# Merging the 64-row query tiles of two heads in an attention and MLP kernel

## The chip, the core and the metric

The kernel runs on one NeuronCore of a Trainium2 chip. The metric is the time of the whole program on the device in microseconds (us). Before the change the median of 3 runs is 1101.58 us.

## The reference

Attention over 4 batches, 8 heads, 576 tokens and 64 features, with a second, memory branch, then two feed-forward layers over all 2304 tokens.

```python
def _attn_ref(q, k, v, M_prev, z_prev, beta):
    scores = scale * np.matmul(q, k.transpose(0, 1, 3, 2))
    scores = np.where(causal, -1000000000.0, scores)
    a = np.exp(scores - scores.max(-1, keepdims=True))
    a /= a.sum(-1, keepdims=True) + 1e-09
    local = np.matmul(a, v)
    q_p = phi(q)                                   # elu + 1
    mem_ret = np.einsum('bhsd,bhde->bhse', q_p, M_prev)
    mem_norm = np.einsum('bhsd,bhd->bhs', q_p, z_prev)[..., None] + 1e-06
    g = 1.0 / (1.0 + np.exp(-beta))[None, :, None, None]
    return g * mem_ret / mem_norm + (1 - g) * local

def _moe_ref(x, w_in, w_out, s, b):
    r = np.maximum(x @ w_in, 0.0)
    return (s * (r * r) + b) @ w_out

def _moe2_ref(x, w_in, w_out, a, b):
    h = x @ w_in
    P = a[0] + a[1] * h + a[2] * h * h + a[3] * h * h * h
    Q = 1.0 + np.abs(b[0]) * np.abs(h) + np.abs(b[1]) * h * h
    return (P / (Q + 1e-06)) @ w_out
```

The weights of the two layers come as 64-bit floats and are decoded on the chip into a high and a low part; d_model is 512 and d_ff 2048.

## The kernel before

Attention is cut into 32 units. A unit is one batch, one pair of heads (`hp`, four of them) and one set of query tiles: **low** units hold tiles 0 to 2 (384 rows), **high** units tiles 3 and 4 (128 rows and 64). The units go batch by batch, four low ones, then four high ones. The two heads of a pair lie in the two halves of the 128 partitions, `j` is the head in the pair, and `n = 2 * p + j` counts unit and head.

Per unit `prepare_qk` and `prepare` load the transposed queries and keys, the values `v`, the memory `mb`, the untransposed queries `qn` and the row `zb`. `scores` (L605) multiplies per head and query tile, 64 rows of the array for each head; the last tile's 576 key columns are cut in two of 288, so that a high unit has four matmuls of 288 columns. One operation of VectorE (DVE) per matmul adds the mask and takes the row maximum (L612), one of ScalarE (ACT) takes the exponential and the row sum (L623). `sums` makes the divisors `rec`. `transposes` (through `turn`, L506) turns the probabilities, 128x128 at a time, into PSUM (`pt`), from where they are copied to `th`; `high_q.trans` lists 5 and 4 of them per head, also those of the 64-row tile. `phi_a` and `phi_b` make the features `ph` of the memory branch and turn them (`pf`). `values` (L753) multiplies the values `vs` with `th`, each head into its half of the columns of the array and of the bank `av`, adds the memory product (L762, one fp32 matmul, or three of split operands from unit `MPLAIN` on), and scales by the divisors `cb` (L765) into `xp`, which is stored to `xTd`. In units below `DIRECT` the divisors are spread on the array (`rb`, `ct`); in the others they go through DRAM, `c1` to `crow` and `crow` to `cb`.

The blocks of the first feed-forward layer (`ha`, L810, and `acc`, L875) need the stored outputs of whole batches. Seven of nine are started while attention still runs, as filling for TensorE (PE).

No order is written out by hand. Every operation is handed to `Plan` with the engines that could do it, a cost for each, its buffers and a due time `at`. `Plan.run` steps through the program with these costs, gives each engine the operation that could start first and, among those, the one with the earlier due time, and issues it. So costs, ring sizes (`RQ`, `RP`, `RT`, `RU`, `RV`) and due times set each engine's order. A transfer on the queue of SyncE (SP) is reckoned like this:

```python
            if e == "SP":
                clock[e] = start + 0.48
                dma = max(dma, start + 1.2) + cost
                o.end = dma + 0.95
```

Of the kernel before, what the change touches and what calls it, by code (L numbers as in the profile page):

```python
# [20 lines left out]
P = 128  # L21
# [22 lines left out]
GROUPS = {2: [[0], [1]], 3: [[0], [1, 2]]}  # L44
# [5 lines left out]
DIRECT, GATE, MPLAIN = 4, 1.0, 8  # L50
# [29 lines left out]
class Plan:  # L80
# [83 lines left out]
    def run(self, engines, nbanks):  # L164
# [40 lines left out]
        for _ in self.ops:  # L205
# [43 lines left out]
def tile_kernel(ctx, tc, qk, vm, z, beta, w1i, w1o, s1, b1, w2i, w2o, a2, b2, out):  # L249
# [46 lines left out]
    for i in range(2):  # L296
        t = at.tile([P, P], F32, name=f"rec{i}")
        nc.gpsimd.memset(t, 0.0)
        buf(f"rec{i}", None, obj=t)
# [12 lines left out]
    gate = cst.tile([P, H], F32, name="gate")  # L312
    omg = cst.tile([P, H], F32, name="omg")
# [5 lines left out]
    for n in ("rec0", "rec1", "wsum"):  # L319
        plan.bufs[n].const = True  # L320
# [21 lines left out]
    def load(dst, src, size, r=(), w=(), act=False):  # L342
# [3 lines left out]
        else:  # L346
            op({"SP": size / 360e3}, lambda e: e.dma_start(dst(), src()), r, w)  # L347
# [26 lines left out]
    def gates():  # L374
# [5 lines left out]
        op(ways(H, None, 1.0), lambda e: e.tensor_scalar(omg, gate, -1.0, 1.0, ALU.mult, ALU.add), ("gate",), ("omg",))  # L380

# [60 lines left out]
    def w1_half(k, pool):  # L442
# [33 lines left out]
        ta=3, tb=4, scores=[(512, [(3, 0, 0, 512, 0)]), (S, [(4, 0, 0, QB, 0), (4, 1, QB, S, QB)])],  # L476
        trans=[[(0, 3, 4), (1, 3, 4), (4, 4, 4)], [(2, 3, 4), (3, 3, 4)]])
# [30 lines left out]
    def prepare_qk(p):  # L508
# [3 lines left out]
        at_ring(f"q{p}", "q", RQ, [P, r.nqt])  # L512
        at_ring(f"k{p}", "k", RQ, [P, r.nk])
        for j in range(2):
            m = slice(j * D, j * D + D)
            load(lambda m=m: g(f"q{p}")[m], lambda j=j, m=m: src[m, j, r.q0:r.q0 + r.nqt], D * 4 * r.nqt, (), ((f"q{p}", j),))
            load(lambda m=m: g(f"k{p}")[m], lambda j=j, m=m: src[m, j, SQ:SQ + r.nk], D * 4 * r.nk, (), ((f"k{p}", j),), p < 2)

    def prepare(p):
# [724 lines left out]
```

## Time and profile before

| | |
|---|---|
| median of 3 runs (lowest, highest) | 1101.58 us (1100.44, 1101.63) |
| the profiled execution's own time | 1095.03 us |
| its span, first to last instruction | 1093.2 us |
| PE busy in the span | 1052.1 us (96%) |
| DVE, ACT, GpSimd (POOL) busy | 856.0, 699.5, 403.9 us |
| mean granted clock of PE | 0.981 |

The profile is of one execution. A busy share counts the time in which at least one instruction of the engine ran; matmuls are pipelined, so their durations overlap. The chain of the work that ended last, merged into pieces, has them end to end. In names of tiles the buffer numbers are left out; an arrow points from what is read to what is written.

### The profile page before, as it was taken

How to read it: one execution, taken by the hardware profiler on the slowest of the kernel's cores; microseconds unless marked ns; L12 is line 12 of the kernel's file. 1: busy time of each engine (PE TensorE's matmuls, PEld its weight loads, DVE VectorE, ACT ScalarE, POOL GpSimd, SP SyncE). 2: the span in 40 equal slices, each digit the busy share in tenths (PEclk: the TensorE clock that was granted, in tenths of full speed). 3: DMA queues.
4: the chain of work that ended last, by engine and by line, in shares of the span. 5: the costliest groups of instructions: out<-in, count | busy, mean ns of one | idle time of the engine just before them, and what ended most of it. 6: DMA issues, size and time to landing. Idle time of an engine off the chain costs nothing.

```text
span 1093.2 us, 17895 instructions
## 1 busy us (share of the span) xinstructions
PE 1052.1 (96%) x6104; PEld 880.4 (81%) x6104; DVE 856.0 (78%) x1560; ACT 699.5 (64%) x1513; POOL 403.9 (37%) x431
## 2 busy tenths in 40 slices
PE   6987989999999999999999999999999999999998
PEld 3566778777887778998777899888888888899997
DVE  5888977787776885579999733788788888887995
ACT  5865765675656674354555433776866876787885
POOL 1201321210111211110111000776876776877785
PEclk8988999999999999999999999999999999999999
DMA  7755566566555562997766302910200100010000
GB/s 197 206 167 164 152 180 186 152 184 184 177 163 158 180 206 89 333 308 255 240 193 220 123 23 75 327 49 0 76 1 1 56 13 1 22 39 1 30 1 29
DMA packets 95547, 140.98 MB, mean 129 GB/s; under 512 B 13144, under 2 KB 59360, under 8 KB 95456
## 3 DMA queue, kind: packets, MB, share of 16 engines
q1 hardware_dynamic: 90912, 131.06, 38.4%
q0 software_dynamic: 4224, 8.39, 2.6%
q8 instruction: 48, 0.79, 0.3%
q10 hardware_dynamic: 320, 0.39, 0.1%
q14 instruction: 43, 0.35, 0.1%
HBM read 104.08 MB, written 35.72 MB: 128 GB/s over the span
## 4 chain that ended last, share of the span: by engine, by line
PE 73%; DVE 10%; DMA 10%; ACT 2%; SPq 2%; issue 2%; POOL 0%; DVEq 0%; ACTq 0%; POOLq 0%
PE ac L1001 18%; PE hc L810 18%; PE acc L875 7%; PE ha L810 7%; PE ab L914 5%; PE hb L810 5%; PE s L605 4%; PE pt L506 3%; PE av L753 3%; SPq L347 2%; DMA cb<-crow 2%; PE av L762 1%; DVE s L612 1%; ACT p L623 1%; DMA d2i_1r<-in_w2i 1%
## 5 line engine op out<-in xcount | busy, mean ns | idle before, releaser
L980 DVE RECIPROCAL qe<-qe 128x512 f32<-128x512 f32 (+2 forms) x82 | 242.7, 2960 | 51.9 <-POOL qe L363 51.8
L363 POOL TENSOR_TENSOR qe<-qe,qb 128x512 f32<-128x512 f32 (+2 forms) x82 | 95.1, 1159 | 65.5 <-ACT qb L965 65.0
L810 PE MATMUL hc<-xc_h,w2il 128*128 128x512 f32 (+1 forms) x320 | 118.7, 371 | 0.0
L810 PE MATMUL hc<-xc_h,w2ih 128*128 128x512 f32 (+1 forms) x320 | 118.6, 371 | 0.0
L810 PE MATMUL hc<-xc_l,w2ih 128*128 128x512 f32 (+1 forms) x320 | 118.4, 370 | 0.0
L1001 PE MATMUL ac<-w2oh,glc 128*128 128x512 f32 x288 | 113.6, 395 | 0.0
L1001 PE MATMUL ac<-w2oh,ghc 128*128 128x512 f32 x288 | 113.4, 394 | 0.0
L1001 PE MATMUL ac<-w2ol,ghc 128*128 128x512 f32 x288 | 113.3, 393 | 0.0
L623 ACT ACTIVATE p<-s,st 128x288 f32<-128x288 f32 (+4 forms) x192 | 97.9, 518 | 18.8 <-DVE st L612 18.0
L363 POOL TENSOR_TENSOR glc<-po,ghc 128x512 fp32r<-128x512 f32 (+2 forms) x82 | 95.0, 1159 | 21.8 <-ACT ghc L353 21.8
L363 POOL TENSOR_TENSOR pm<-pm,s 128x512 f32<-128x512 f32 (+2 forms) x82 | 95.4, 1163 | 12.6 <-ACT pm L965 11.5
L605 PE MATMUL s<-k,q 64*128 64x288 f32 (+4 forms) x384 | 83.8, 490 | 16.6 <-DMA q<-in_qk 4.4
L875 PE MATMUL acc<-gha,w1olA 128*128 128x256 f32 x288 | 86.9, 302 | 0.0
L971 ACT ACTIVATE s<-hc 128x512 f32<-128x512 f32 (+2 forms) x82 | 44.6, 544 | 65.8 <-PE hc L810 62.8
L875 PE MATMUL acc<-gla,w1ohA 128*128 128x256 f32 x288 | 82.6, 287 | 3.2 <-DVE gla L828 3.2
L875 PE MATMUL acc<-gha,w1ohA 128*128 128x256 f32 x288 | 82.5, 286 | 0.0
L612 DVE CUSTOM_DVE_ANT_0 s<-s,mask 128x128 f32<-128x128 f32 (+4 forms) x160 | 74.2, 503 | 10.5 <-PE s L605 8.2
L506 PE MATMUL pt<-ident,p 128*128 128x128 f32 x480 | 69.8, 284 | 11.9 <-ACT p L623 4.8
L506 PEld LDWEIGHTS pt<-ident,p 128*128 128x128 f32 x480 | 54.9, 145 | 26.3 <-issue 8.1
L965 ACT ACTIVATE pm<-hc,prm 128x512 f32<-128x512 f32 (+2 forms) x82 | 59.5, 726 | 22.1 <-DVE hc L982 21.7
L605 PEld LDWEIGHTS s<-k,q 64*128 64x128 f32 x384 | 40.1, 199 | 37.2 <-issue 9.6
L810 PEld LDWEIGHTS hc<-xc_l,w2ih 128*128 128x128 f32 x320 | 60.1, 188 | 9.4
(472 smaller groups left out, 2933.2 us busy)
## 6 DMA issues: line engine op xcount, KB each, us to landing
v<-in_vm SPq DMA_DIRECT2D x16, 320.0 KB
k<-in_qk SPq DMA_DIRECT2D x32, 144.0 KB
x2p<-ev SPq DMA_DIRECT2D x18, 256.0 KB
out_y<-ob SPq DMA_DIRECT2D x18, 256.0 KB
w1d<-sh SPq DMA_DIRECT2D x16, 256.0 KB
w1d<-sl SPq DMA_DIRECT2D x16, 256.0 KB
w2d<-sh SPq DMA_DIRECT2D x16, 256.0 KB
w2d<-sl SPq DMA_DIRECT2D x16, 256.0 KB
```

The lines of the kernel that those rows point to most:

```text
L363: op(ways(c, None, dve, pool), lambda e: e.tensor_tensor(dst(), x(), y(), alu), r, w, port=True)
L506: nc.tensor.transpose(dst[:, o:o + P], src, ident)
L605: nc.tensor.matmul(g(b)[:, o2:o2 + kb - ka], g(Q)[m, q], g(K)[m, ka:kb], start=True, stop=True)
L612: e.tensor_tensor_reduce(sp, sp, mask[:, m0:m0 + kb - ka], -scale, 3.0e38 if x == 0 else st[:, t:t + 1], ALU.add, ALU.min, st[:, t + x:t + ...
L623: e.activation(g(f"p{n}_{i}")[:, o:o + kb - ka], g(b)[:, o2:o2 + kb - ka], AF.Exp, scale=-1.0, bias=g(f"st{n}")[:, z_:z_ + 1], accum_out=g ...
L810: nc.tensor.matmul(hs(), m, y, start=c == 0 and k == 0, stop=c == KC - 1 and k == 2)
L875: nc.tensor.matmul(a, outp(y, f)[:, cs], g(z_)[:, us], start=f == 0 and k == 0 and c % 2 == 0, stop=f == HF - 1 and k == 2, skip_group_che ...
L914: nc.tensor.matmul(g(ACC)[:, 0:w], outp(y, f)[:, cs], g(z_), start=f == 0 and k == 0, stop=f == HF - 1 and k == 2)
L965: return lambda e: e.activation(g(dst)[:, ks], g(src)[:, ks], AF.Identity, scale=m, bias=b)
L971: op(ways(c, -0.04), lambda e, ks=ks: e.activation(g(S2)[:, ks], g(HS)[:, ks], AF.Square), (HS,), part(S2))
L980: op({"DVE": 0.07 + c * 0.00625}, lambda e, ks=ks: e.reciprocal(g(QE)[:, ks], g(QE)[:, ks]), part(QE), part(QE))
L1001: nc.tensor.matmul(g(ACC), g(x_)[:, ks], g(f"w2o{y}{i}")[:, o], start=f == 0 and q == 0, stop=f == NF - 1 and q == 2)
```

## The change

In high units the 64 rows of tile 4 of both heads become one tile of 128 rows. `diagonal` copies the two 64x64 pieces of the queries on POOL into a block-diagonal `qd`, two of which lie ready with zeros. `scores_last` multiplies it with all 128 rows of the keys, two matmuls of 288 columns in place of four, with one masked reduction and one exponential each into `su` and `pu`; `mask2` is the mask of the second half. `transposes_last` turns per block of 128 keys head 0's tile 3, the merged tile and head 1's tile 3 together, 13 transposes per unit and not 18. In `values` a key block then gives head 0 one matmul of 192 columns and head 1 one of 64 and one of 128. `phi_b` turns the two masked halves of tile 4's features by a matmul with `both`, two identities side by side; `gate2` holds the gates with zeros.

Loads are joined: memory with values (high) or with untransposed queries (low), `zb` for two units, `crow` for both heads in low units; high queries are loaded without the unused 64 rows. The planner reckons a fixed part per transfer, 128 columns for each transpose, half as much for matmuls in `values`, and 250 columns more where the memory product follows them. `MPLAIN` goes from 8 to 4, `RP` from 8 to 7, `RU` from 4 to 1; `rb` shares the ring of `xp`.

```diff
-RQ, RP, RT, RU, RV = 3, 8, 8, 4, 1
+RQ, RP, RT, RU, RV = 3, 7, 8, 1, 1
-DIRECT, GATE, MPLAIN = 4, 1.0, 8
+DIRECT, GATE, MPLAIN = 4, 1.0, 4
-                o.end = dma + 0.95
+                o.end = dma + 1.2
-            op({"SP": size / 360e3}, lambda e: e.dma_start(dst(), src()), r, w)
+            op({"SP": 0.1 + size / 350e3}, lambda e: e.dma_start(dst(), src()), r, w)
...
+    def diagonal(p):
+        Q, QD = f"q{p}", f"qd{p % 2}"
+        for j in range(2):
+            m = slice(j * D, j * D + D)
+            op({"POOL": 0.2}, lambda e, m=m: e.tensor_scalar(g(QD)[m, m], g(Q)[m, P:P + 64], 1.0, 0.0, ALU.mult, ALU.add),
+               (Q,), ((QD, j),))
...
+    def scores_last(p):
+        Q, K, RS, ST, PR = f"qd{p % 2}", f"k{p}", f"rs{p}", f"su{p}", f"pu{p}"
...
+            def mm(SB=SB, ks=ks):
+                nc.tensor.matmul(g(SB)[:, 0:QB], g(Q), g(K)[:, ks], start=True, stop=True)
+            pe(4.5 * QB, mm, (Q, K), (SB,))
+            op(ways(QB, None, 1.0), lambda e, SB=SB, x=x: e.tensor_tensor_reduce(
+                g(SB)[:, 0:QB], g(SB)[:, 0:QB], mask2 if x else mask[:, 0:QB], -scale,
+                g(ST)[:, 0:1] if x else 3.0e38, ALU.add, ALU.min, g(ST)[:, x:x + 1]), (SB, (ST, 0)) if x else (SB,), (SB, (ST, x)))
+        for x in range(2):
+            op(ways(QB, 0.15), lambda e, SB=f"su{p}_{x}", x=x: e.activation(
+                g(PR)[:, x * QB:x * QB + QB], g(SB)[:, 0:QB], AF.Exp, scale=-1.0, bias=g(ST)[:, 1:2],
+                accum_out=g(RS)[:, x, 5:6]), (f"su{p}_{x}", (ST, 1)), ((PR, x), (RS, (x, 5, 0))))
...
-            pe(2 * w, tr, src, (PT,))
+            pe(2 * P * len(todo), tr, src, (PT,))
...
+    def transposes_last(p, kbs):
+        for kb in kbs:
+            parts = [(f"p{2 * p}_0", kb), (f"pu{p}", kb), (f"p{2 * p + 1}_0", kb)] + [(f"pu{p}", 4)] * (kb == 0)
...
+            for j, o, ra, rb in ((0, 0, 0, 192), (1, 192, 128, 192), (1, 256, 0, 128)):
+                runs.append((kb, j, kb, TH, o, ra, rb))
+            if kb == 0:
+                for j in range(2):
+                    runs.append((kb, j, 4, TH, 384 + 64 * j, 128, 192))
...
-            pe(4 * sum(rb - ra for _, _, _, ra, rb in part) + 100 * len(part), mm,
+            pe(2 * sum(x[6] - x[5] for x in part) + 50 * len(part), mm,
...
-        pe((3 if r.split_m else 4) * w, mem, (AV, FS, f"ml{p}", f"mh{p}", f"fl{p}") if r.split_m else (AV, MB, FS), (AV,))
+        pe((3 if r.split_m else 4) * w + 250, mem, (AV, FS, f"ml{p}", f"mh{p}", f"fl{p}") if r.split_m else (AV, MB, FS), (AV,))
```

The planner's order moves with this on every engine. Three places show it.

The first is PE at the scores of unit 15, a high one. `s30` and `s31` are the two heads' scores, `pt28` and `pt29` the transposed probabilities of unit 14's two heads, `pf14` its features. Before:

```order
L605 MATMUL s30_0_0_2802<-k15_2262,q15_2249 128x512
L605 MATMUL s31_0_0_2803<-k15_2262,q15_2249 128x512
L506 MATMUL pf14_2808<-ident_74,ph14_2402 128x128 x2
L675 MATMUL pf14_2808<-ident_74,rec0_84 128x128
L605 MATMUL s30_1_0_2814<-k15_2262,q15_2249 128x288
L605 MATMUL s31_1_0_2815<-k15_2262,q15_2249 128x288
L506 MATMUL pt29_0_2824<-ident_74,p29_0_2656 128x128
L506 MATMUL pt29_0_2824<-ident_74,p29_1_2708 128x128
...
L605 MATMUL s30_1_1_2851<-k15_2262,q15_2249 128x288
L605 MATMUL s31_1_1_2852<-k15_2262,q15_2249 128x288
```

The same place now, with the merged scores `su15`:

```order
L521 MATMUL pf14_2749<-ident_74,ph14_2372 128x128
L732 MATMUL pf14_2749<-both_100,ph14_2372 128x64
L742 MATMUL pf14_2749<-ident_74,rec0_92 128x128
L644 MATMUL s30_0_0_2753<-k15_2246,q15_2238 128x512
L644 MATMUL s31_0_0_2754<-k15_2246,q15_2238 128x512
L678 MATMUL su15_0_2770<-k15_2246,qd1_98 128x288
L678 MATMUL su15_1_2775<-k15_2246,qd1_98 128x288
L521 MATMUL pt28_2_2782<-ident_74,p28_0_2592 128x128
L521 MATMUL pt28_2_2782<-ident_74,pu14_2628 128x128
L521 MATMUL pt28_2_2782<-ident_74,p29_0_2608 128x128
```

Four matmuls of 288 columns in two places have become two in one place, directly behind the scores of tile 3, and the transposes behind them take both heads of unit 14 in one.

The second is PE at the values of unit 14. `th28` and `th29` are its two heads before, `vs14` its values. Before:

```order
L753 MATMUL av14_2889<-th28_0_2800,vs14_2492 64x192
L753 MATMUL av14_2889<-th29_0_2859,vs14_2492 64x192
L753 MATMUL av14_2889<-th28_0_2800,vs14_2492 64x192
L753 MATMUL av14_2889<-th29_0_2859,vs14_2492 64x192
L753 MATMUL av14_2889<-th28_0_2800,vs14_2492 64x64
L753 MATMUL av14_2889<-th29_0_2859,vs14_2492 64x64
```

Now, where `th28_0` to `th28_3` are the four key blocks of both heads, and matmuls of the first layer (`ha2`) stand between the second and the third block:

```order
L852 MATMUL av14_2812<-th28_0_2747,vs14_2478 64x192
L852 MATMUL av14_2812<-th28_0_2747,vs14_2478 64x64
L852 MATMUL av14_2812<-th28_0_2747,vs14_2478 64x128
L852 MATMUL av14_2812<-th28_0_2747,vs14_2478 64x64 x2
L852 MATMUL av14_2812<-th28_1_2757,vs14_2478 64x192
L852 MATMUL av14_2812<-th28_1_2757,vs14_2478 64x64
L852 MATMUL av14_2812<-th28_1_2757,vs14_2478 64x128
L909 MATMUL ha2_2_2829<-xa2h0_2111,w1ilA_388 128x256
```

The two heads no longer alternate with equal widths, and the values of one unit stand in two pieces.

The third is DVE at the same scores of unit 15, before:

```order
L612 ISA s30_1_0_2814,st30_2812<-s30_1_0_2814,mask_75 128x288
L612 ISA st30_2812 128x1
L612 ISA s31_1_0_2815,st31_2820<-s31_1_0_2815,mask_75 128x288
L612 ISA st31_2820 128x1
L545 TENSOR_SCALAR ph16_2857<-qn16_2552 128x384
L612 ISA s30_1_1_2851,st30_2812<-s30_1_1_2851,mask_75,st30_2812 128x288
L612 ISA st30_2812 128x1
L612 ISA s31_1_1_2852,st31_2820<-s31_1_1_2852,mask_75,st31_2820 128x288
```

and now:

```order
L681 ISA su15_0_2770,su15_2801<-su15_0_2770,mask_75 128x288
L681 ISA su15_2801 128x1
L367 COPY th28_2_2808<-pt28_2_2782 128x384
L681 ISA su15_1_2775,su15_2801<-su15_1_2775,mask2_84,su15_2801 128x288
L681 ISA su15_2801 128x1
```

Four reductions over 288 columns, each with its read of the accumulator, are two, and a copy of transposed probabilities stands between them.

## Rows read from the trace of the kernel before

**Rows 1.** Busy time by stretch of 50 us, 0 to 200 us.

```profile
core 0: us, PE busy (x) PEld busy (x) DVE busy (x) ACT busy (x) POOL busy (x), PEclk, DMA share, GB/s
0.00:50.00 50.00, 37.55 (x188) 22.47 (x190) 35.17 (x126) 35.66 (x107) 10.68 (x27) 0.86 0.69 194
50.00:100.00 50.00, 41.62 (x265) 31.86 (x262) 44.74 (x111) 31.12 (x77) 7.16 (x12) 0.83 0.61 178
100.00:150.00 50.00, 45.03 (x329) 36.18 (x328) 42.48 (x140) 34.59 (x105) 14.74 (x22) 0.96 0.53 159
150.00:200.00 50.00, 47.41 (x376) 39.88 (x375) 38.46 (x114) 28.78 (x77) 8.77 (x18) 1.00 0.60 180
```

**Rows 2.** Busy tenths of PE in 40 equal slices of the span.

```profile
PE   6987989999999999999999999999999999999998
```

**Rows 3.** Busy time by stretch of 10 us, and the sum to 440 us.

```profile
90.00:100.00 10.00, 8.61 (x32) 7.28 (x33) 9.81 (x19) 5.22 (x13) 3.53 (x3) 0.50 0.55 171
...
250.00:260.00 10.00, 7.91 (x47) 6.30 (x49) 9.53 (x28) 7.45 (x23) 1.49 (x2) 0.83 0.48 156
...
sum 440.00, PE 403.80 PEld 322.49 DVE 337.79 ACT 280.41 POOL 74.89; mean PE 9.18 PEld 7.33 DVE 7.68 ACT 6.37 POOL 1.70
```

**Rows 4.** PE's waits before 440 us: total us, times, longest us.

```profile
PE pt L506 <- ACT p L623: 4.8, 1, 4.8
...
PE acc L875 <- DVE gla L828: 3.2, 1, 3.2
PE s L605 <- DVE xp L765: 2.9, 3, 1.4
```

**Rows 5.** The chain that ended last, merged: start us, length us, what.

```profile
300.56 0.92 PE av L753 x12
301.47 0.69 PE s L605 x4
302.16 0.80 PE av L753 x8
...
313.46 0.98 PE pt L506 x9
...
321.15 1.57 PE av L753 x20
...
435.46 1.57 PE av L753 x20
```

**Rows 6.** PE in order of time: start us, length us, at 78.9 us.

```profile
78.93 0.59 PE L762 MATMUL av<-fs,mb 128*128 128x192 f32 x2
79.23 0.42 PE L875 MATMUL acc<-gha,w1olA 128*128 128x256 f32 x1
79.48 0.28 PE L875 MATMUL acc<-gla,w1ohA 128*128 128x256 f32 x1
```

**Rows 7.** PE in order of time, behind scores at 269.5 us.

```profile
270.41 0.39 PE L875 MATMUL acc<-gha,w1olA 128*128 128x256 f32 x1
270.64 0.28 PE L875 MATMUL acc<-gla,w1ohA 128*128 128x256 f32 x1
270.76 0.28 PE L875 MATMUL acc<-gha,w1ohA 128*128 128x256 f32 x1
```

**Rows 8.** DVE groups, 0 to 460 us: count, busy us, mean ns, idle before.

```profile
L612 DVE DVE_READ_ACCUMULATOR2_ANT st<- 128x1 f32 x192 | 26.9, 140 | 0.0
...
L612 DVE CUSTOM_DVE_ANT_0 s<-s,mask,st 128x288 f32<-128x288 f32 x32 | 15.7, 520 | 0.2 <-PE s L605 0.2
L612 DVE CUSTOM_DVE_ANT_0 s<-s,mask 128x288 f32<-128x288 f32 x32 | 14.4, 477 | 0.0
```

**Rows 9.** ACT groups, 0 to 460 us.

```profile
L623 ACT ACTIVATION_READ_ACCUMULATOR p<-s,st 128x1 f32 x192 | 38.7, 202 | 0.0
L623 ACT ACTIVATE p<-s,st 128x288 f32<-128x288 f32 x64 | 31.2, 500 | 3.2 <-DVE st L612 3.0
```

**Rows 10.** POOL group, 0 to 460 us.

```profile
L569 POOL TENSOR_SCALAR vs<-v,omg 128x192 f32<-128x192 f32 x12 | 6.2, 523 | 30.0 <-PE av L753 24.2 <-PE pt L506 4.5 <-DMA v<-in_vm 1.3
```

**Rows 11.** SP's queue in order of time: start us, length us of one issue.

```profile
44.08 0.53 SPq L347 DMA_DIRECT2D zb<-in_z  x1
```

More of the change, by code (lines that the diff above doesn't have):

```diff
@@ L43 @@
 ALONE = 8
-GROUPS = {2: [[0], [1]], 3: [[0], [1, 2]]}
 R0, R1, RN = 0.0, 0.0, 0
@@ L295, in tile_kernel @@
     )
-    for i in range(2):
-        t = at.tile([P, P], F32, name=f"rec{i}")
+    mask2 = at.tile([P, QB], F32, name="mask2")
+    nc.vector.memset(mask2, 0.0)
+    for j in range(2):
+        m = mask2[j * 64:j * 64 + 64, QB - 64:]
+        nc.gpsimd.affine_select(m, m, pattern=[[-1, 64]], compare_op=ALU.is_ge, fill=-2.0e9 / scale, base=0, channel_multiplier=1)
+    for n in ("rec0", "rec1", "qd0", "qd1"):
+        t = at.tile([P, P], F32, name=n)
         nc.gpsimd.memset(t, 0.0)
-        buf(f"rec{i}", None, obj=t)
+        buf(n, None, obj=t)
+    both = at.tile([P, 64], F32, name="both")
+    nc.vector.tensor_tensor(both, ident[:, 0:64], ident[:, 64:128], ALU.add)
     wsum = cst.tile([P, DM], F32, name="wsum")
@@ L312, in tile_kernel @@
     gate = cst.tile([P, H], F32, name="gate")
+    gate2 = cst.tile([P, H, 2], F32, name="gate2")
+    nc.vector.memset(gate2, 0.0)
+    buf("gate2", None, obj=gate2)
     omg = cst.tile([P, H], F32, name="omg")
@@ L663, in phi_t @@
         def phi_t():
-            for j in range(r.ta, r.tb + 1):
+            for j in range(r.ta, r.tb + (r.tb < NQ - 1)):
                 flip(g(PT), q0s[j] - r.q0, g(F)[:, j - r.ta, :], j)
+            if r.tb == NQ - 1:
+                nc.tensor.matmul(g(PT)[:, P:P + 64], g(F)[:, 1], both, start=True, stop=True)
         def along(dst, o1):
@@ L721, in transposes @@
                 qa = q0s[ta] - r.q0
[L722 to L723 removed]
+                runs.append((i, j, kb, f"th{n}_{i}", o, qa, qa + w - o))
             TH = f"th{n}_{i}"
[L725 removed]
+            at_ring(TH, "th", RT, [P, w])
             def tr(PT=PT, todo=todo):
@@ L1047, in tile_kernel @@
         events.append((t - AHEAD if p >= RQ else TS - AHEAD + 0.001 * p, lambda p=p: prepare_qk(p)))
-        events.append((t - AHEAD + 0.01, lambda p=p: prepare(p)))
-        events.append((t, lambda p=p: (scores(p), sums(p))))
+        events.append((t - AHEAD + 0.01, lambda p=p: (prepare(p), diagonal(p) if units[p].r.tb == NQ - 1 else None)))
+        events.append((t, lambda p=p: (scores(p), scores_last(p) if units[p].r.tb == NQ - 1 else None, sums(p))))
         for j in range(2):
-            events.append((t + (VAL + 0.1 * j) * d, lambda p=p, j=j: runs.update({p: transposes(2 * p + j)})))
+            events.append((t + (VAL + 0.1 * j) * d, lambda p=p, j=j: runs.setdefault(p, []).extend(transposes(2 * p + j))))
         events.append((t + 0.1, lambda p=p: phi_a(p)))
```

149 lines of the change are left out of this document (93 added, 56 removed).

## The prediction

> **What bounds the kernel now.** I read the table of stretches first [rows 1], then the row of slices [rows 2], and the two together give the picture. In the slices TensorE (PE) is at nine tenths or more from the seventh of 40 on, save the last; from 440 us, where attention ends, nothing but the expert layers is left, 650 us that the change leaves as they are. The attention units lie before. In 0 to 150 us PE is busy 37.55, 41.62 and 45.03 us of 50, so it stands idle 12.4, 8.4 and 5.0 us, at a mean clock of 0.86, 0.83 and 0.96 [rows 1]; VectorE (DVE) is the fullest of the others there, 44.74 of 50 in the second stretch. In 150 to 200 us PE is busy 47.41 and DVE 38.46. PE's idle time to 440 us is 36.2 us in all [rows 3], so only 10.4 us of it come after 150. There each microsecond of PE work taken from attention is nearly a microsecond of the span: PE executes in order, matmuls of the first expert layer stand between the attention pieces, and what follows moves up. Before 150 us it is worth only what the chain through DVE and ScalarE (ACT) lets through. The list of PE's waits [rows 4] says what the gaps wait for: an exponential once for 4.8 us, DVE's gla once for 3.2. No single repeated wait is there to be removed.
>
> What one matmul takes on PE can't be read from mean durations, because they contain the pipeline. I take it from the merged chain [rows 5], whose pieces stand end to end.
>
> **The change part by part.** Sixteen of the 32 attention units are high ones (query tile 3, and tile 4 with only 64 rows). Everything of size happens there.
>
> *Transposes.* 18 of 128x128 per high unit become 13. Nine take 0.98 us [rows 5], 0.109 us each: 5 x 0.109 x 16 = **8.7 us less** on PE. The copies out of PSUM stay four per unit, with the same 1664 columns.
>
> *Scores of tile 4.* Before, two pairs of 64-row matmuls over 288 columns, a pair in 0.69 us [rows 5], its heads partly side by side. Now two single 128-row matmuls. A pair is four instructions, of which I take three to stand end to end (the first head's two, the second head's last): 0.23 us each. A single matmul is two of them one after the other, 0.46 us. That is 1.38 against 0.92: 0.46 x 16 = **7.4 us less**. The ends are 0 (each still costs 0.69) and 0.48 per unit, by the 192-column fp32 matmul with the memory, from 78.93 to 79.23 [rows 6], so 0.45 us for 288 columns.
>
> *Values.* Before, the heads come in pairs of equal width in the two column halves: two pairs of 192 take 0.80 us, two of 192 and one of 64 take 0.92, the five of a unit 1.57 [rows 5]. That fits two instructions per matmul, started in order, each of 0.83 ns per column and holding its half: a pair of 192 then adds 0.32 us and the last instruction hangs over by 0.16. Now each key block has one of 192 in one half, then 64 and 128 in the other. The next 192 can't start before the second instruction of the 128 does, so by the same count a block adds 0.373 in place of 0.32, and a unit takes about 1.77: 0.2 x 16 = **3.2 us more**. The ends are 0 (1.57 stays) and no overlap at all: 1664 columns at 0.30 us per 192 [rows 6] are 2.6 us, 1.03 x 16 = 16.5 us more. I stay near the low end, because all three rows agree with the count.
>
> *Switching.* Where PE goes from one kind of matmul to another, the steady 0.12 us from start to start is broken: 270.41 to 270.64 after the scores, then 270.76 [rows 7]; 79.23 to 79.48 after the memory [rows 6]. That is about 0.1 us extra each. In the order of PE the attention part has 296 changes of kind before and 320 after: 24 x 0.1 = **2.4 us more**, between 0 and twice that. The Trainium skill (TensorEngine Tiling (Array Packing), Key Properties) says that changing the tiling mode drains the engine, which speaks against this change; the rows agree that a switch costs, with 0.1 us. By the rule alone the change is worse by 24 drains; no row here prices a drain apart from that 0.1.
>
> *Small ones on PE.* Units 4 to 7 go from one fp32 matmul with the memory, 0.30 us [rows 6], to three split ones, at 0.12 us or a little more each [rows 7], 0.4 in all: 4 x 0.1 = **0.4 us more**. The flip of tile 4's features, 0.109 us, becomes a 64-column fp32 matmul, by the memory's row a third of 0.30: nothing.
>
> PE altogether: -8.7 - 7.4 + 3.2 + 2.4 + 0.4 = **-10.1 us**.
>
> *DVE and ACT.* The 64 masked reductions over 288 columns become 32: half of 14.4 + 15.7 us, and 32 accumulator reads of 0.14 us [rows 8]: 19.5 us less on DVE. The exponentials over 288 columns halve too: half of 31.2 us, and 32 reads of 0.2 us [rows 9]: 22 us less on ACT. Against that the four newly split units each add a cast and two subtractions, of 128 and 192 columns; at most 0.49 us each, by the 288-column row [rows 8], so 3.9 us on DVE, and I take 2.5. None of this is on PE; it pays only through PE's waits. In 50 to 150 us, where units 4 to 7 run, those are 13.4 us, and DVE loses 5 of 87 busy us there and gains 2.5 back. From 150 to 440 us the waits are 10.4 us. I take **5 us less** waiting, half of it in each part. The ends are 0 and 23.8 us (all of it).
>
> *GpSimd (POOL).* It gets two 64x64 copies per high unit, which build the block-diagonal queries. The nearest row is its scaling of 192 columns, 523 ns [rows 10], so at most 32 x 0.52 = 17 us on an engine busy 7 to 15 of 50 [rows 1]. A copy stands in its queue behind what waits there for DVE and ACT; the merged score matmul stands behind the copy, and all of PE behind that. The planner puts the copies 5 us ahead of the unit; I cost them at nothing on that cover. Without it each unit's copies are a PE wait of about 0.5 us, 8 us over 16 units.
>
> *Transfers.* Some 60 queue issues of 722 fall away. Each holds the queue of SyncE (SP) for about 0.5 us, as the issue of zb does with 0.53 [rows 11], with nearly the same bytes behind them. The queue gets ahead by that, but the loads are issued units ahead, and the two hops of the divisors through DRAM (crow, then cb) remain. The new costs let the planner place later on DVE what waits for cb. Both are inside the 5 us. The ring sizes (one buffer for the first transposed block; the divisors' ring shared with the outputs) would bite only if a unit's first values came after the next unit's transposes; in the order they come before.
>
> **The sum.** -10.1 - 5 = -15.1 us. The profiled execution took 1095.03 us, 6.55 below the median of the runs shown, 1101.58. The one gives 1079.9, the other **1086.5**, which I forecast, with 1081 to 1092 for this case alone. A measurement of this kernel can tell about 0.2%, 2.2 us, from no change. Chance of this case: 0.50.
>
> **The rivals.**
> *A. The early gaps close too.* If PE's waits in 50 to 150 us mostly go, and with them the half-speed stretch (90 to 100 us stands at 0.50, so 8.6 busy us do the work of 4.3 [rows 3]), another 6 to 13 us fall: 1073 to 1081. For it: DVE is near full there and loses reductions. Against: the weight decoding, which fills it, stays. Chance 0.17.
>
> *B. The saved work turns into waiting.* PE arrives earlier at pieces whose inputs come at DVE's and ACT's pace, or waits for POOL's copies (8 us above). Half of the gain or more goes: 1092 to 1099.4 for a gain that still shows (0.15), 1099.4 to 1103.8 for none (0.07). For it: the waits come from many places [rows 4], and a new order draws them anew. Against: those engines lose more work than PE does.
>
> *C. Slower: the clock falls between the pieces.* After a gap PE runs a stretch at 1.2 GHz in place of 2.4: in 250 to 260 us it stands idle 2.1 us, and the mean clock is 0.83 [rows 3], which costs another 1.3 of its 7.9 busy us. With less PE work per unit, a high unit that is held by a late POOL copy could open such a gap each time, at 3.4 us. From 6 of the 16 units on this eats the 15.1 us and the 2.2 of a measurement; at 8 units it is 27.2 us more, 1113.7. For it: such a dip is there in 250 to 260 us, and a longer one in 90 to 100. Against: DVE and ACT, which PE would wait for, lose some 20 us each. The Trainium skill (TensorE: Matmul & The Clock Gate, Part 1) has the throttled state as the default, released by activity; the rows agree in that the low clock stands beside idle time. Chance 0.11.
>
> That the change does not do what it says is hardly possible here: the counts of instructions fall as stated in the order of the changed kernel.
>
> **How the numbers follow.** Faster by over 0.2%: 0.50 + 0.17 + 0.15 = 0.82; within it 0.07; slower 0.11. For 8 in 10 I leave out C, B's no-gain and the end of A below 1074: 1074 to 1100.
>
> **What would show it.** The nine-transpose pieces become pieces of four and three at 0.109 us each. Two merged scores take about 0.92 us, and no pair of 288 is left. The values of a high unit take about 1.8 us; 2.6 would mean that the halves no longer overlap. DVE's busy time is some 17 us lower and ACT's some 20. The last values, at 435.46 us now [rows 5], come near 420. I am wrong if PE's idle time to the end of attention grows past its 36 us of now, if a wait of the merged scores for POOL stands among PE's longest, or if a stretch after 150 us shows a clock near 0.5.

## The result, and the profile after

| | before | after |
|---|---|---|
| median (lowest, highest) | 1101.01 us (1095.56, 1101.63), 4 runs | 1072.25 us (1071.45, 1072.85), 4 runs |
| the profiled execution | 1095.03 us, span 1093.2 | 1071.45 us, span 1069.7 |
| mean granted clock | 0.981 | 0.989 |

The ratio is 0.9765, with an interval of 0.9736 to 0.9794: faster by 2.1 to 2.6%. From profiled execution to profiled execution it is 23.6 us, against the 15.1 of the forecast. All readings below are of the profiled executions.

The page's row of engines and its row of slices, after:

```profile
PE 1029.7 (96%) x6108; PEld 864.4 (81%) x6108; DVE 847.0 (79%) x1528; ACT 689.3 (64%) x1460; POOL 398.9 (37%) x442
...
PE   6889899999999999999999999999999999999998
```

PE lost 22.4 busy us of 1052.1, nearly the whole gain. DVE lost 9.0 and ACT 10.2.

The stretches of 50 us and of 10 us that answer to [rows 1, 3], and then the whole stretch from 0 to the last attention matmul. The columns are the length, then busy time and count of PE, PE's weight loads, DVE, ACT and POOL, then clock, DMA share and GB/s:

```profile
0.00:50.00 50.00, 36.69 (x179) 22.07 (x179) 35.07 (x129) 34.19 (x104) 15.50 (x44) 0.88 0.68 203
50.00:100.00 50.00, 44.37 (x351) 35.13 (x351) 45.76 (x122) 36.02 (x95) 14.22 (x20) 0.91 0.64 188
100.00:150.00 50.00, 42.92 (x312) 34.01 (x311) 43.53 (x124) 32.94 (x91) 10.46 (x23) 0.97 0.54 162
150.00:200.00 50.00, 48.24 (x396) 40.02 (x394) 38.69 (x118) 30.46 (x78) 8.44 (x17) 1.00 0.61 184
...
90.00:100.00 10.00, 9.46 (x85) 7.84 (x84) 9.75 (x27) 7.99 (x25) 1.63 (x3) 1.00 0.57 181
...
250.00:260.00 10.00, 10.00 (x70) 7.44 (x69) 8.36 (x26) 7.01 (x18) 0.48 (x2) 1.00 0.56 179
...
0.00:415.37 415.37, 380.40 (x2914) 304.67 (x2915) 329.77 (x989) 269.43 (x731) 76.86 (x160) 0.97 0.59 179
```

The same stretch of the kernel before:

```profile
0.00:437.38 437.38, 401.18 (x2920) 319.87 (x2920) 337.42 (x1028) 279.76 (x785) 74.89 (x142) 0.95 0.58 172
```

Attention ends 22.0 us earlier; behind it 1.5 us change. PE's idle time up to there is nearly what it was: 36.2 us before, 35.0 after. So the gain is in PE's busy time, and a part of that is the clock. The two low clocks of [rows 3], 0.50 at 90 us and 0.83 at 250 us, have gone. All in all, before, half the clock (1.2 GHz in place of 2.4) was granted in seven stretches up to the end of attention, at 15, 32, 56, 90, 144, 254 and 342 us. After, it is four. Here are the 10 us before the third of them, then the four with their sum, and last the sum of the seven before:

```profile
60.00:70.00 10.00, 5.72 (x56) 4.33 (x52) 8.83 (x28) 5.82 (x13) 1.75 (x3) 0.95 0.85 214
...
14.39:24.63 10.24, 7.31 (x25) 4.02 (x26) 8.54 (x36) 8.63 (x27) 3.30 (x7) 0.50 0.58 165
48.52:51.94 3.42, 3.42 (x14) 1.64 (x14) 1.74 (x6) 1.87 (x8) 2.02 (x4) 0.50 0.45 170
69.00:75.83 6.83, 5.74 (x27) 5.48 (x28) 4.99 (x14) 5.30 (x16) 2.11 (x4) 0.50 0.47 123
120.20:123.62 3.42, 3.42 (x11) 1.91 (x10) 3.38 (x12) 2.03 (x7) 0.20 (x1) 0.50 0.64 196
sum 23.91, PE 19.89 PEld 13.04 DVE 18.66 ACT 17.83 POOL 7.63; mean PE 4.97 PEld 3.26 DVE 4.66 ACT 4.46 POOL 1.91
...
sum 40.96, PE 37.55 PEld 24.93 DVE 39.69 ACT 27.43 POOL 8.66; mean PE 5.36 PEld 3.56 DVE 5.67 ACT 3.92 POOL 1.24
```

PE was busy for 37.55 us at half clock before and for 19.89 after. Half of that is what the low clock costs, 18.8 and 9.9 us. The stretch at 69 us stands at the end of 10 us in which PE idled 4.3.

The pieces of the merged chain after, which answer to [rows 5] (start, length, what):

```profile
178.13 0.77 PE pt L521 x7
178.90 0.11 PE pf L521
179.00 0.17 PE pf L732 x2
179.17 0.12 PE pf L742
179.29 1.06 PE s L644 x4
180.35 1.17 PE su L678 x4
181.52 0.67 PE pt L521 x6
...
412.36 0.94 PE av L852 x14
413.30 0.91 PE acc L974 x6
414.20 0.82 PE av L852 x10
415.02 0.51 PE av L861 x3
```

PE's longest waits before 440 us, which answer to [rows 4], with the longest wait of merged scores (`su`):

```profile
PE pt L521 <- ACT th L365: 7.0, 8, 2.0
PE pf L521 <- ACT p L662: 4.8, 2, 4.3
PE s L644 <- DMA k<-in_qk: 4.3, 2, 3.7
PE pt L521 <- ACT p L662: 4.2, 2, 3.8
...
PE su L678 <- ACT fs L365: 1.7, 1, 1.7
```

The groups of the merged tile up to 460 us, which answer to [rows 8, 9, 10]:

```profile
L685 ACT ACTIVATE pu<-su,su 128x288 f32<-128x288 f32 x32 | 15.8, 503 | 1.9 <-DVE su L681 1.4
...
L539 POOL TENSOR_SCALAR qd<-q 64x64 f32<-64x64 f32 x32 | 10.8, 339 | 56.3 <-DMA q<-in_qk 30.6 <-PE su L678 24.8
...
L681 DVE CUSTOM_DVE_ANT_0 su<-su,mask,su 128x288 f32<-128x288 f32 x16 | 8.3, 519 | 0.3
```

**An account of PE.** To compare kernels whose clocks dip in different places, I split the time to the end of attention (the start of the first matmul behind the last one of attention) three ways. *Idle* is that time less PE's busy time. *Slow* is what the half clock costs: over all of PE's matmuls, the time from a start to the next start, less idle time, times one less the clock that was granted in just that time. That matmuls take about twice as long at half clock shows in the values of one unit before: 2.97 us in the stretch at 56 us, 1.57 at full clock. The rest is *work* at full clock. It is of one execution for each kernel.

| | end | idle | slow | work |
|---|---|---|---|---|
| before | 437.4 | 36.2 | 18.8 | 382.4 |
| after | 415.4 | 35.0 | 9.9 | 370.5 |
| difference | -22.0 | -1.2 | -8.9 | -11.9 |

By kind, in us at full clock:

| kind of matmul | before | after | measured | forecast |
|---|---|---|---|---|
| transposes (`pt`) | 54.8 | 47.2 | -7.6 | -8.7 |
| scores (`s`; after `s` and `su`) | 74.7 | 50.0 + 17.6 | -7.1 | -7.4 |
| values | 49.8 | 53.0 | +3.2 | +3.2 |
| product with the memory | 16.6 | 16.9 | +0.3 | +0.4 |
| flip of features (`pf`) | 14.4 | 15.5 | +1.1 | 0 |
| spread of divisors (`ct`) | 1.6 | 1.8 | +0.2 | 0 |
| first layer (`ha`, `acc`) | 170.5 | 168.5 | -2.0 | +2.4 for all switching |

Two things were open. Which part of the gain belongs to the merged tile, and which to the joined loads and the planner's costs? And is the smaller part, idle and slow time, an effect of anything in the change, or the luck of a new order?

### The profile page after: what moved, and what is told of

Read it like the earlier page. It is cut to its first block, busy times and chain, and to the rows that moved or that the text cites. A ratio compares the mean times of both kernels' runs of the same rounds, so it can differ in the third digit from the quotient of the medians.

```text
span 1069.7 us, 17742 instructions
## 1 busy us (share of the span) xinstructions
PE 1029.7 (96%) x6108; PEld 864.4 (81%) x6108; DVE 847.0 (79%) x1528; ACT 689.3 (64%) x1460; POOL 398.9 (37%) x442
## 4 chain that ended last, share of the span: by engine, by line
PE 68%; DVE 7%; DMA 6%; ACT 2%; SPq 2%; issue 1%; POOL 0%; DVEq 0%; ACTq 0%; POOLq 0%
PE ac L1100 19%; PE hc L909 19%; PE ab L1013 7%; PE hb L909 7%; PE acc L974 5%; PE ha L909 5%; PE av L852 2%; SPq L359 2%; PE s L644 1%; PE pt L521 1%; DMA cb<-crow 1%; DMA k<-in_qk 1%; DMA xTd<-xp 1%; DVE s L651 1%; PE av L861 1%
## 5 line engine op out<-in xcount | busy, mean ns | idle before, releaser
L375 POOL TENSOR_TENSOR pm<-pm,s 128x512 f32<-128x512 f32 (+2 forms) x82 | 95.8, 1168 | 16.4 <-ACT pm L1064 15.5
L974 PE MATMUL acc<-gha,w1olA 128*128 128x256 f32 x288 | 84.5, 293 | 0.0
L662 ACT ACTIVATE p<-s,st 128x128 f32<-128x128 f32 (+3 forms) x128 | 66.6, 527 | 19.9 <-DVE st L651 18.8
L1064 ACT ACTIVATE pm<-hc,prm 128x512 f32<-128x512 f32 (+2 forms) x82 | 59.5, 725 | 19.6 <-DVE hc L1081 19.1
L521 PE MATMUL pt<-ident,p 128*128 128x128 f32 x320 | 59.8, 286 | 12.3 <-ACT th L365 7.0
L909 PEld LDWEIGHTS hc<-xc_h,w2il 128*128 128x128 f32 x320 | 60.1, 188 | 9.4 <-DVE po L1083 0.2
L651 DVE CUSTOM_DVE_ANT_0 s<-s,mask 128x128 f32<-128x128 f32 (+3 forms) x128 | 60.3, 508 | 9.0 <-PE s L644 8.0
L909 PEld LDWEIGHTS hc<-xc_h,w2ih 128*128 128x128 f32 x320 | 60.1, 188 | 8.6
L365 ACT COPY th<-pt 128x384 f32<-128x384 f32 (+1 forms) x117 | 54.6, 496 | 18.3 <-PE pt L521 18.2
```

The costliest lines, as they stand in the source:

```text
L365: e.copy(dst(), src())
L375: op(ways(c, None, dve, pool), lambda e: e.tensor_tensor(dst(), x(), y(), alu), r, w, port=True)
L521: nc.tensor.transpose(dst[:, o:o + P], src, ident)
L651: e.tensor_tensor_reduce(sp, sp, mask[:, m0:m0 + kb - ka], -scale, 3.0e38 if x == 0 else st[:, t:t + 1], ALU.add, ALU.min, st[:, t + x:t + ...
L662: e.activation(g(f"p{n}_{i}")[:, o:o + kb - ka], g(b)[:, o2:o2 + kb - ka], AF.Exp, scale=-1.0, bias=g(f"st{n}")[:, z_:z_ + 1], accum_out=g ...
L909: nc.tensor.matmul(hs(), m, y, start=c == 0 and k == 0, stop=c == KC - 1 and k == 2)
```

## The experiments

None of them leaves out a part of the computation. They ran on three occasions; on these the kernel before had medians of 1097.74 us (the first four), 1095.82 (the next four) and 1097.64 us (the last four), and the ratios are to those. The theory was first that the merged tile alone carries the gain.

**The merge taken back.** The tile of 64 rows is computed per head again; the joined loads, the costs and `MPLAIN` 4 stay (`RP` is 8 for the additional tiles).

```diff
-RQ, RP, RT, RU, RV = 3, 7, 8, 1, 1
+RQ, RP, RT, RU, RV = 3, 8, 8, 1, 1
-        ta=3, tb=4, scores=[(512, [(3, 0, 0, 512, 0)])], trans=[])
+        ta=3, tb=4, scores=[(512, [(3, 0, 0, 512, 0)]), (S, [(4, 0, 0, QB, 0), (4, 1, QB, S, QB)])],
+        trans=[[(0, 3, 4), (1, 3, 4), (4, 4, 4)], [(2, 3, 4), (3, 3, 4)]])
...
-        events.append((t, lambda p=p: (scores(p), scores_last(p) if units[p].r.tb == NQ - 1 else None, sums(p))))
+        events.append((t, lambda p=p: (scores(p), sums(p))))
```

> The changed kernel with the 64-row tiles of the two heads kept apart as before (four score matmuls of 288 columns, 18 transposes, ring RP at 8); joined loads, planner costs, MPLAIN 4 stay. Theory (the gain is PE work of the merge, about 14 us, plus clock and waits that come with it): 1092 to 1101 us, median near 1096. Rival (planner costs and transfers carry the clock and the waits, the merge only its PE work): 1084 to 1088 us.

Measured: 1096.04 us, ratio 0.9985 (0.9962 to 1.0008), where the theory had its median. To the end of attention:

```profile
0.00:435.56 435.56, 389.43 (x2921) 314.64 (x2921) 349.17 (x1054) 279.80 (x781) 80.86 (x142) 0.97 0.57 172
```

Without the merge nothing that can be measured is left of the gain in this order (another order is measured below). The account gives work of 378.2 us, idle 46.1, slow 11.3: the work is 7.7 us over that of the changed kernel, and there are 12.5 us more of idle and slow time.

**The planner's old costs.** Everything else of the change stays.

```diff
-                o.end = dma + 1.2
+                o.end = dma + 0.95
-            op({"SP": 0.1 + size / 350e3}, lambda e: e.dma_start(dst(), src()), r, w)
+            op({"SP": size / 360e3}, lambda e: e.dma_start(dst(), src()), r, w)
...
-            pe(2 * P * len(todo), tr, src, (PT,))
+            pe(2 * w, tr, src, (PT,))
...
-        pe((3 if r.split_m else 4) * w + 250, mem, (AV, FS, f"ml{p}", f"mh{p}", f"fl{p}") if r.split_m else (AV, MB, FS), (AV,))
+        pe((3 if r.split_m else 4) * w, mem, (AV, FS, f"ml{p}", f"mh{p}", f"fl{p}") if r.split_m else (AV, MB, FS), (AV,))
```

> The changed kernel with the old planner costs: 0.95 us after a transfer and no fixed part, transposes by valid columns, nothing for the tiling change. Theory (merge): 1070 to 1076 us, the clock share redrawn by a few us. Rival (the planner's costs carry the part that was not forecast, 8 to 13 us): 1080 to 1086 us.

The lines left out price the flips of the features and the spread of the divisors in the same way. The price of the matmuls in `values` stays, and that leaves no part of the change in: the halved factors now stand for one head's matmul where they stood for both heads', so for a matmul the price is the old one.

Measured: 1089.98 us, 0.9926 (0.99 to 0.9953), beyond what even the rival had.

```profile
0.00:434.65 434.65, 387.81 (x2915) 312.19 (x2915) 332.48 (x994) 269.10 (x729) 76.91 (x157) 0.95 0.56 171
...
DVE xp L864 <- DMA cb<-crow: 12.1, 10, 2.3
```

The work is 368.7 us, as low as in the changed kernel, but 46.8 idle and 19.1 slow us go with it. The theory that the merged tile alone carries the gain fell: the merge takes the work off PE, and whether this shows depends on the order. DVE's wait for the divisors through DRAM, in the last row, was 9.2 us before and is 7.2 in the changed kernel.

**The joined loads issued apart.** Memory and values (or queries), `zb` and `crow` are loaded as before, and the unused rows of the queries with them, from the same places into the same buffers.

```diff
-            load(lambda: g(f"vm{p}"), lambda: tiles[:, 0:NQ + 1], P * 512 * (NQ + 1), (), (f"vm{p}",))
+            load(lambda: g(f"vm{p}")[:, 0:NQ], lambda: tiles[:, 0:NQ], P * 512 * NQ, (), ((f"vm{p}", 0),))
+            load(lambda: g(f"vm{p}")[:, NQ], lambda: tiles[:, NQ], P * 512, (), ((f"vm{p}", 1),))
```

> The changed kernel with the joined transfers issued apart again (memory from values, memory from queries, zb per unit, crow per head, unused query rows loaded). Theory: 1071 to 1076 us, since the loads are early. Rival (SP's queue holds the first 100 us back): 1077 us or more, with PE's idle time up to 150 us grown by 4 us or more.

Measured: 1078.0 us, 0.9823 (0.9781 to 0.9865). By its time the rival holds, by its place it doesn't:

```profile
0.00:50.00 50.00, 36.80 (x196) 22.35 (x197) 39.56 (x144) 35.62 (x106) 17.00 (x39) 0.90 0.76 208
50.00:100.00 50.00, 41.04 (x303) 33.07 (x302) 45.24 (x119) 31.77 (x80) 16.85 (x20) 0.90 0.65 195
100.00:150.00 50.00, 46.42 (x347) 36.60 (x346) 43.90 (x130) 34.01 (x100) 11.29 (x24) 0.93 0.54 159
...
0.00:420.60 420.60, 380.65 (x2915) 305.41 (x2916) 333.53 (x995) 265.84 (x719) 91.87 (x166) 0.97 0.60 178
```

PE is busy 124.3 us of the first 150, as in the changed kernel (124.0). The 5 us are lost behind that, 14.2 us idle against 9.0. The intervals of the two ratios overlap; what the joined loads are worth is not settled.

**Values head by head.** Of the high units, blocks 0 and 1 and then blocks 2 and 3 are taken in one group each, head 0's matmuls first, then head 1's, so that the column halves can't alternate.

```diff
-        for i in sorted({x[0] for x in runs}):
-            part = [x for x in runs if x[0] == i]
-            if r.tb < NQ - 1:
-                part.sort(key=lambda x: (x[2], x[1]))
+        groups = [[i] for i in sorted({x[0] for x in runs})] if r.tb < NQ - 1 else [[0, 1], [2, 3]]
+        for i, ii in enumerate(groups):
+            part = [x for x in runs if x[0] in ii]
+            part.sort(key=(lambda x: (x[2], x[1])) if r.tb < NQ - 1 else (lambda x: x[1]))
```

> The changed kernel with the values of high units in two groups of two key blocks, in each group all matmuls of head 0 and then all of head 1, so that the column halves work one after the other but for the seam. Theory (the halves overlap, started in order, 0.83 ns per column and instruction): the two pieces of a unit take 1.4 and 1.2 us in place of 0.94 and 0.82, so 0.8 us more per unit and 13 us in all, 1082 to 1088 us. Rival (unequal widths hardly overlap in the changed kernel anyway): no more than 3 us slower, 1072 to 1076 us.

Measured: 1081.77 us, 0.9849 (0.9805 to 0.9893). In the merged chain:

```profile
306.94 1.31 PE av L852 x15
309.51 0.83 PE av L852 x10
...
421.40 1.31 PE av L852 x15
423.97 0.83 PE av L852 x10
```

The time lies just under the 1082 to 1088 of the theory, but not for its reason: it had 1.4 and 1.2 us for the two groups. The first takes 1.31 us in place of 0.94. The second takes 0.83, as long as before, where a count in order of start gives 1.1 or more. So the overlap of the halves exists and is worth 0.37 us in one group, but the count in order is wrong. The starts show why. These are the values' matmuls in 0.03 us from the start of a second group, and in 0.21 us from the start of a first one (columns: PE, its weight loads, clock, DMA share, GB/s):

```profile
309.43:309.46 0.03, 0.02 (x2) 0.02 (x2) 1.00 1.25 341
306.86:307.07 0.21, 0.20 (x1) 0.19 (x2) 1.00 0.72 249
```

Each matmul stands in the profile as two instructions. In the second groups head 0 has four, and head 1's first starts 0.01 us after head 0's first, before the three others. In the first groups head 0 has six, and head 1's first starts 0.38 us after head 0's first, right behind the third. So each half works through its own matmuls at its own pace, and the other half's can start ahead of the program's order, here by four places in both kinds of group, in all 15 of each that are not cut up.

By kind the values cost 5.2 us more than in the changed kernel. Attention ends 9.7 us later, and by the account only 2.8 of these are work, 1.9 idle and 5.1 slow time: most of it is the order again.

At this point each edit, even a small one, had cost 5 to 24 us. That made the rival serious that the changed kernel's order is a lucky draw. A number that moves due times a little and means nothing for the time gives other orders of the same kernel: `LAG`, the delay with which stored outputs are counted as there, and the first of `TIMES`, from which the due times of the units are made.

**The changed kernel and the kernel before, in another order; and the old costs once more.**

```diff
-LAG, AHEAD, LOADS, EARLY = 18.0, 5.0, 10.0, 7
+LAG, AHEAD, LOADS, EARLY = 18.6, 5.0, 10.0, 7
```

> The changed kernel with one due-time number moved a little (LAG 18.0 to 18.6), which draws the whole order anew and changes no work. Theory D (PE's work is 14 us less whatever the order; idle time and slow clock, 44 us in the changed kernel, are a draw that comes out between 44 and 66): some place in 1070 to 1092 us, with PE's work before the end of attention at 371 us within 2. Theory P (the planner's costs fix them): 1070 to 1077 us.

> The kernel before with the same number moved. Theory D: off the kernel before by up to 12 us either way (1086 to 1110 on the scale of this chip's 1098), with PE's work at 386 us within 2. Theory P says the same of a kernel with the old costs.

> The changed kernel with the old planner costs and the same number moved. Theory D: 1072 to 1092 us, and it need not be slower than the new costs with the number moved. Theory P: 1084 us or more, and at least 8 us slower than the new costs with the number moved.

Measured: the changed kernel 1073.13 us, 0.9783 (0.9719 to 0.9846). The kernel before 1104.07, 1.007 (1.004 to 1.0099). The changed kernel with the old costs 1092.62, 0.9959 (0.9936 to 0.9983). All three stay in their places, the last 19.5 us behind the first, which was theory P's mark, so it is not a draw alone. The work that was expected, 386 us for the kernel before and 371 for the changed one, each within 2, was missed: it is 381.2 and 368.7.

**The changed kernel with `TIMES` moved.**

```diff
-TIMES = 8.5, 8.0, 1.2
+TIMES = 8.6, 8.0, 1.2
```

> The changed kernel with another due-time number moved (TIMES 8.5 to 8.6): a third draw with the new costs. Theory D: 1070 to 1092 us; with the two others it shows how wide the draw is. Theory P: 1070 to 1077 us.

Measured: 1063.58 us, 0.9693 (0.9639 to 0.9748), the best of the study and below what either theory had.

```profile
0.00:406.23 406.23, 376.51 (x2914) 307.23 (x2915) 331.15 (x974) 264.65 (x717) 96.15 (x189) 0.97 0.60 183
...
DVE xp L864 <- DMA cb<-crow: 4.9, 8, 1.2
```

Its work, 368.8 us, is that of the others; idle (29.7) and slow time (7.8) are the smallest of all. So a draw can be worth some 9 us, and a part must be worth more than that to be credited from one pair of runs.

**The two kinds of costs apart.** First only the two lines on transfers are the old ones, then only those on PE (cut to one).

```diff
-                o.end = dma + 1.2
+                o.end = dma + 0.95
-            op({"SP": 0.1 + size / 350e3}, lambda e: e.dma_start(dst(), src()), r, w)
+            op({"SP": size / 360e3}, lambda e: e.dma_start(dst(), src()), r, w)
```

> The changed kernel with the old costs for transfers alone (0.95 us after the last byte, no fixed part); the new costs of PE's operations stay. If the transfers' costs are what the other draws with old costs missed: 1086 to 1093 us, with idle time and slow clock before the end of attention at 58 us or more. If PE's costs are: 1068 to 1078 us, with 38 to 49 us.

```diff
-            pe(2 * P * len(todo), tr, src, (PT,))
+            pe(2 * w, tr, src, (PT,))
```

> The changed kernel with the old costs of PE's operations alone (transposes by valid columns, nothing for the tiling change); the new costs for transfers stay. If the transfers' costs decide: 1068 to 1078 us. If PE's do: 1086 to 1093 us. If both are needed: over 1078 in both this run and the one with the old transfer costs.

Measured: with the old transfers 1081.22 us, 0.9846 (0.9815 to 0.9877); with PE's old costs 1070.72, 0.9759 (0.9726 to 0.9793). The first lies between its two expectations, the second within the one by which the transfers decide. PE's costs are worth nothing that shows by themselves. The transfers' old price goes with 9 us, which is as much as a draw, and only both old together (1090 and 1093) lose the 18 to 20. Why PE's costs matter only there stays open.

**`TIMES` moved in the kernel without the merge, and in the kernel before.**

> The kernel with the tiles kept apart and all else of the change, with TIMES at 8.6, the draw that was the best for the merged one. If the new costs pay in any kernel: 1076 to 1086 us (PE's work of about 381 us and some 44 of idle time and slow clock). If they pay only with the merge: 1091 to 1102 us, as in the first unmerged draw.

> The kernel before with TIMES at 8.6. If the 8 us that this number gave the changed kernel are its own virtue: 1086 to 1092 us. If they were a draw: 1093 to 1106 us, like the two others of the kernel before.

Measured: without the merge 1088.04 us, 0.9915 (0.9886 to 0.9944), between the two expectations. The kernel before 1099.94, 1.0026 (1.0004 to 1.0048): the number is no virtue in itself. But it took some 8 us off both kernels with the new costs, so that it suits these is not excluded.

**All accounts together** (us; the account is of the profiled execution, whose time stands beside the median and can lie up to 6 us from it; "DMA" is what DVE and ACT wait for transfers before 440 us, added up from the list of waits):

| kernel | median | profiled | work | idle + slow | DMA |
|---|---|---|---|---|---|
| before | 1101.01 | 1095.03 | 382.4 | 55.0 | 72.7 |
| before, `LAG` moved | 1104.07 | 1098.83 | 381.2 | 59.9 | 77.9 |
| before, `TIMES` moved | 1099.94 | 1099.96 | 380.9 | 59.4 | 81.1 |
| not merged | 1096.04 | 1091.92 | 378.2 | 57.4 | 52.4 |
| not merged, `TIMES` moved | 1088.04 | 1087.3 | 381.6 | 49.4 | 59.8 |
| merged, both costs old | 1089.98 | 1093.53 | 368.7 | 65.9 | 98.1 |
| merged, both costs old, `LAG` moved | 1092.62 | 1089.55 | 367.8 | 58.7 | 86.2 |
| merged, transfers' costs old | 1081.22 | 1081.17 | 365.9 | 54.4 | 85.5 |
| after | 1072.25 | 1071.45 | 370.5 | 44.9 | 71.9 |
| after, `LAG` moved | 1073.13 | 1073.37 | 368.7 | 48.4 | 58.4 |
| after, `TIMES` moved | 1063.58 | 1064.08 | 368.8 | 37.5 | 57.8 |
| after, PE's costs old | 1070.72 | 1071.27 | 368.6 | 43.1 | 64.0 |
| after, loads apart | 1078.0 | 1076.29 | 369.5 | 51.1 | 73.6 |
| after, values head by head | 1081.77 | 1083.73 | 373.3 | 51.9 | 62.3 |

The work falls into two classes: 378.2 to 382.4 us in the five kernels without the merge, on average 380.9, and 365.9 to 370.5 in the eight with it (head by head left out), on average 368.6. So **the merge takes some 12 us of work from PE, in every order**: the classes lie 7.7 us apart where they are nearest. In the two pairs that differ in the merge alone, and `RP` with it (not merged against after, with each `TIMES`) it is 7.7 and 12.8.

Idle and slow time does not divide as cleanly. Without the merge it is 56.2 us on average, 58.1 with the old costs and 53.4 with the new. With the merge it is 59.7 in the three kernels with the old price of transfers, and 43.5 in the four from "after" to "PE's costs old"; the two with other edits and the new price, the last rows, lie between with 51.1 and 51.9.

The times say the same more plainly. With the new costs the merge is worth 24 us (1096.04 against 1072.25, 1088.04 against 1063.58), twice the work that it takes off PE. With the old ones the changed kernel is only 8 to 11 us ahead of the kernel before, though its loads are joined too. The costs together are worth 18 to 20 us in the merged kernel, over two orders each. How they share this rests mostly on one order each: the transfers' price is worth 9 us beside PE's new costs and 19 beside the old ones, PE's costs 9 us beside the transfers' old price and nothing beside the new. **That the price of transfers is the larger part is likely by this, and not shown**, since a draw alone is worth 9.

The waits of DVE and ACT for transfers go with that price: 72.7 us and more in all six kernels with the old one, 73.6 and less in the eight others. The changed kernel itself, with 71.9, stands at that border, and the kernel without the merge has the fewest (52.4) with 57.4 us of idle and slow time. That the shorter waits are the way by which idle and slow time fell is not shown.

## Why the prediction was right, step by step

The forecast came in its direction and its main term: faster, from PE's work in the high units, -11.9 us for the -10.1 of the sum, with the last values at 414.20 us where I had "near 420". The size did not. The measured ratio on the median I started from, 0.9765 x 1101.58, is 1075.7 us; the median itself, 1072.25, lies 1.75 under the low end of the range. Both are below the 1081 to 1092 that I gave the forecast case alone, and 1075.7 is in the range of rival A. The sum was 8.5 us too small from execution to execution, and the part that it lacks is the clock.

- *Transposes*, right, if not in full (-7.6 for -8.7): pieces of seven (four and three) take 0.77 us and six 0.67, 0.110 us each, where I had 0.109.
- *Scores*, right: -7.1 for -7.4 us. Both prices were too low by about the same: two merged matmuls cost 1.10 us on average, 17.6 / 16, where I said 0.92, and an old pair 0.77, (74.7 - 50.0) / 32, and not the 0.69 of the one piece that I read in [rows 5]. A unit saves 0.44, where I had 0.46.
- *Values*, right in the number, and by luck, since the reason was another: 0.94 + 0.82 us against 1.77, +3.2 us over all. The end of 2.6 us without overlap is refuted. But the unequal widths hardly cost. In a merged kernel, here with PE's old costs, the values of a unit that stand in one piece take 1.61 us, from their start to the next matmul's (three more at full clock in these runs do; a fifth halts inside and takes 1.77):

```profile
81.58 1.68 PE L852 MATMUL av<-th,vs 128*64 128x192 f32 x28 [0.57 <-ACT th L365]
83.19 0.38 PE L909 MATMUL ha<-xa0h,w1ilA 128*128 128x256 f32 x1
```

  That is 0.04 over the 1.57 of [rows 5]. In two pieces they take 1.76, and the kernel before took 0.92 + 0.80 = 1.72 where it had two [rows 5]. So what costs is the second piece, 0.15 us. The 16 high units have 21 pieces before and 36 after; 15 x 0.15 + 16 x 0.04 = 2.9 us is an estimate of the whole from this. My count took the matmuls to start in the program's order, and the head-by-head kernel refutes that: the column halves do not wait for each other in this way, and "PE executes in order" does not hold between them.
- *Switching*, +2.4 us, can't be seen apart. Without that term I had -12.5 us for PE. The attention pieces came to -9.9, so 2.6 dearer, and the first layer to -2.0, of which nine matmuls fewer at 0.12 us are 1.1. Pieces contain their own change (the merged scores' 0.18 us over 0.92 is of that kind), so a price for changes beside them counts some twice. And the 24 are changes of kind: the active rows and columns of the array, as the profile gives them for each matmul, change 178 times before and 195 after, 17 more. The Trainium skill (TensorEngine Tiling (Array Packing), Key Properties) has a drain at each change of the tiling mode; no run here tells whether drains are in the 2.6 us.
- *Small ones*: memory +0.3 for +0.4; the flips +1.1 for nothing, for the one through `both` takes 0.17 us in the chain where the transpose took 0.11.
- *DVE and ACT*: the halved rows came as counted (32 reductions of 0.50 us, 32 exponentials of 0.503). But over the whole span busy time fell by 9.0 and 10.2 us, not by 17 and 20. By the page's counts (1560 and 1528) DVE has 32 instructions fewer, where the halving alone makes 64, and POOL 11 more (431 and 442), where the copies alone make 32. So the planner handed other work over; I had held its choice of engines fixed.
- **"I take 5 us less waiting"** is the step that was mis-sized most. Idle time fell by 1.2 us. Slow time fell by 8.9, for which the sum had no term; the clock stood in rivals A and C alone. And "Both are inside the 5 us", said of the freed queue and of the planner's transfer costs, is too little: with the transfers' old costs the changed kernel is 9 us slower, with PE's old costs too 18 to 20. How much of the 8.9 is the change's own is open: in the three orders of the changed kernel slow time is 7.8 to 14.5 us, in the five kernels without the merge 11.3 to 18.8.
- *POOL*, right: a copy takes 0.339 us, below the bound of 0.52, and no wait of the merged scores for POOL is among PE's longest: theirs are 1.7 and 0.9 us, both for ACT.
- *Rival A* came true in its time and half true in its reason. The half clock at 90 us is gone, and with it 4.4 of the 8.9 us; two short ones after 250 us, which it did not name, are another 3.4. But another one stands at 69 to 76 us, and the gaps from 50 to 150 us are 12.7 us, as before 13.4. So that the time falls into its range is partly luck.
- *Rival B* is what the changed kernel does with the old costs: work of 368 us, and 59 to 66 us of idle and slow time, 1090 to 1093. The planner's new costs kept it away here, and I had them inside the 5 us.
- *Rival C* did not come: behind 124 us no stretch at half clock is left. The Trainium skill (TensorE: Matmul & The Clock Gate, Part 1) has the low clock as the state from which activity releases the engine; the stretch at 69 us, at the end of 10 us in which PE idled 4.3, is in line with it.

Left open: what the joined loads and `MPLAIN` do by themselves. `MPLAIN` 8 was not tried in the changed kernel, since there the memory shares the one buffer of the values and would have to outlive it.

## What to carry to other kernels

Read a merge of tiles by the work that it takes off the bounding engine at full clock, which the order moves little, and keep that engine's idle and slow time in another column, since every edit in a planned kernel draws that anew. Before a part is credited or blamed, move a meaningless number and see how far the time goes: here 9 us, as much as most single parts are worth. And a planner whose costs are too low can give back as waiting what a merge saves: here the merge was worth 24 us with the mended costs and at most 11 with the old.

## What was not expected of the hardware

The amount of idle time does not tell how much of the clock is lost. Without the merge 46.1 idle us go with 11.3 slow ones; in the changed kernel with the old transfers' costs it is 38.0 and 16.4, and in the kernel before 36.2 and 18.8. Where the gaps lie decides, by up to 11 us (7.8 to 19.1 over the runs above).

The two column halves of the array do not keep the program's order between them. In the head-by-head kernel two matmuls in one half and then four in the other take 0.83 us, as long as the alternating group of the changed kernel (0.82), because the second half starts 0.01 us after the first and not behind it. With three matmuls in the first half the second starts 0.38 us later, and the group takes 1.31 in place of 0.94. Both are a lead of four instructions; a longer one does not stand in its groups. What does cost is to take the values up again: 0.15 us for a second piece, against 0.04 for unequal widths.
